# First v products early, DMA transposes in place of matmuls, and weights loaded once, in a one-core attention and gated-MLP kernel

## The chip, the cores and the metric

The kernel runs on one core of a Trainium2 chip. The metric is the device time of one execution in microseconds (us). The profile names the engines: PE (matrix products), PEld (its weight loads, beside PE), DVE (vector), ACT (scalar), POOL, and SP, which here only issues transfers. A "span" in a profile is some 1.7 to 2 us shorter than the timed execution.

## The reference, cut to what matters

```python
x = A_x                                    # 2048 tokens x 1024
xn = _layernorm(x, axis=-1)
s = _A_ref(xn, A_wqkv, A_wo)               # 32 heads, 8 keys per query at distances 0, 2, .. 14
g = _silu(_B_ref(xn, B_w1, B_w3, B_w2))    # silu(xn@w1) * (xn@w3) @ w2, inner size 3584
return x + s * g
```

## The kernel before

All large products are done by a Winograd form of Strassen's scheme: seven products of half size in place of eight, from sums of operands that DVE makes. PE is nearly always busy; everything else is arranged around it. Tokens come in four blocks of 512. Two blocks are the two halves of a Strassen product, so the sums of tokens (`xs`) need the second block normalized and transposed as well. Two of a product's seven parts need the first block alone. They are done first, for q and k, and their results parked (`snap`):

```python
for t, (w0, w1_, ws) in enumerate(((wq0, wq1, sq), (wk0, wk1, sk))):
    first_two(f"f{t}", [qkv_A(w0, w1_, ws, g) for g in range(2)], B0[0], B0[1],
              snap[2 * t:2 * t + 2], [qkv_copy(t, 0, 2 * g) for g in range(2)],
              *((lambda: None, 4) if t == 0 else (lambda: tp1(2, 3), 0)))   # tp1: transposes by matmuls
    if t == 0:
        tp1(0, 1)
```

Then follow the other five parts of q and k, all seven of v, the same for the second two blocks, and the MLP. One group of seven goes like this (cut):

```python
def seven(key, A, B, e11, e12, e22, e21, snap=None):
    ...                              # pa: a11*b11, pe: s1*t1; pb starts as a copy of pa
    e11(pa)                          # in the MLP: ACT writes silu(pa) into h_sb
    flush()
    for i in I:
        mm(pb[:, i], s2[i], t2, False)
    su2 = k4(f"u{key}")
    act_copy(su2[:], pb[:])          # ACT, in its order behind e11's activation
    for i in I:
        mm(pe[:, i], s4[i], b22, False)
    e12(pe, su2)
    run_hooks()
    for i in I:
        mm(pb[:, i], s3[i], t3, False)   # adds to pb: must wait for the copy above
    e22(pb, sp5)
```

The outputs of q, k and v for later blocks go through small buffers (`k4`, four of them) to HBM.

## Time and profile before

| | before |
|---|---|
| time, median of 6 runs | 732.54 us (732.24 to 732.9) |
| span of the profiled run | 730.3 us |
| PE busy | 714.2 us, 98% |
| DVE busy | 624.2 us, 85% |

Lines of this profile stand in the prediction below. The columns are start and end, length, busy time of PE, PEld, DVE, ACT and POOL (with the number of instructions), granted clock of PE, DMA share and GB/s:

```profile
600.00:700.00 100.00, 99.74 (x460) 45.38 (x464) 92.46 (x79) 25.27 (x25) 12.12 (x20) 1.00 0.51 160
```

PE is busy for all but 0.26 us there, and DVE for 92 of 100. It is the attention of the last block that DVE does beside PE.

### The profile page before, as it was taken

The page shows a single profiled execution, that of the slowest core. Times are in us where ns is not written, and L with a number is a line of the kernel's source. Part 1 is how long each engine was busy: PE and PEld are TensorE (multiplying, and loading weights), DVE is VectorE, ACT ScalarE, POOL GpSimd, SP SyncE. Part 2 cuts the span into 40 slices and gives each one's busy share as a digit, 9 for nine tenths or more (in the row PEclk, how much of TensorE's full clock was granted, in tenths as well). Part 3 has the DMA queues.
Part 4 walks back from the last instruction along what each step waited for, and adds up shares of the span by engine and source line. Part 5 has one row for each costly group of instructions (what it writes and reads, how often), then busy time and mean ns, then how long its engine had stood idle before and what let it go on. Part 6 is the DMA issues. An engine that isn't in the chain of part 4 may idle for free.

```text
span 730.3 us, 8739 instructions
## 1 busy us (share of the span) xinstructions
PE 714.2 (98%) x3312; PEld 345.8 (47%) x3367; DVE 624.2 (85%) x677; ACT 314.5 (43%) x328; POOL 99.3 (14%) x159
## 2 busy tenths in 40 slices
PE   7999999999999999999999999999999999999996
PEld 4655665654444444444444444444444444444442
DVE  7994688878798879878989899969859999979984
ACT  5744343437554546654545411123454555120233
POOL 0000000010400110142202010010345000510011
PEclk9999999999999999999999999999999999999999
DMA  9379148877756452467755745549799453666505
GB/s 321 140 177 286 57 147 281 254 210 262 200 204 231 143 175 87 141 194 242 231 174 191 240 156 186 178 162 375 188 283 326 136 159 102 192 190 203 179 5 111
DMA packets 117610, 140.82 MB, mean 193 GB/s; under 512 B 14273, under 2 KB 91073, under 8 KB 116929
## 3 DMA queue, kind: packets, MB, share of 16 engines
q1 hardware_dynamic: 103984, 101.47, 44.9%
q0 software_dynamic: 13584, 38.81, 17.2%
q8 instruction: 26, 0.43, 0.3%
q14 instruction: 16, 0.12, 0.1%
HBM read 98.30 MB, written 38.80 MB: 188 GB/s over the span
## 4 chain that ended last, share of the span: by engine, by line
PE 71%; DVE 18%; DMA 4%; issue 3%; ACT 3%; SPq 1%; POOL 0%; DVEq 0%; ACTq 0%; POOLq 0%
PE bm L149 17%; PE am L149 11%; PE em L149 11%; PE db L149 7%; PE bq L149 5%; PE de L149 4%; DVE pt L410 4%; PE eq L149 4%; PE da L149 3%; PE aq L149 3%; PE wb L149 2%; DVE pt L412 2%; PE we L149 2%; PE wa L149 2%; DMA q_dram<-pk 1%
## 5 line engine op out<-in xcount | busy, mean ns | idle before, releaser
L149 PEld LDWEIGHTS <-wring 128*128 128x128 f16 (+1 forms) x1920 | 201.7, 105 | 216.4 <-issue 5.2
L149 PEld LDWEIGHTS <-h_sb 128*128 128x128 f16 (+1 forms) x1088 | 114.0, 105 | 121.7 <-issue 1.0
L149 PE MATMUL bm<-xs,wring 128*128 128x512 f16 x504 | 117.3, 379 | 0.5 <-DVE h_sb L661 0.3
L149 PE MATMUL am<-xT,wring 128*128 128x512 bf16 x322 | 78.8, 379 | 0.9
L410 DVE TENSOR_TENSOR pt<-qt,kT 128x4096 bf16<-128x4096 bf16 x32 | 73.2, 2288 | 0.7
L149 PE MATMUL db<-wring,h_sb 128*128 128x512 f16 x336 | 73.2, 379 | 0.0
L465 DVE TENSOR_TENSOR BC<-Ep,vT 128x2048 bf16<-128x2048 bf16 x56 | 67.0, 1218 | 0.2
L646 DVE TENSOR_TENSOR um<-em,um 128x1024 f32<-128x1024 f32 x28 | 34.2, 1222 | 19.9 <-PE em L149 12.9
L648 ACT ACTIVATE g<-um 128x1024 bf16<-128x1024 f32 x28 | 29.6, 1057 | 49.7 <-DVE um L646 49.7
L149 PE MATMUL da<-wring,h_sb 128*128 128x512 bf16 x219 | 48.9, 379 | 0.3
L451 POOL DMA_DIRECT2D Ep<-pb x64 | 37.9, 600 | 25.5 <-DVE pb L447 18.5
L149 PE MATMUL bm<-h_sb,wring 128*128 128x512 f16 x168 | 39.7, 379 | 0.0
L149 PE MATMUL em<-xs,wring 128*128 128x512 f16 x168 | 39.7, 379 | 0.0
L412 DVE TENSOR_TENSOR pt<-pt 128x2048 bf16<-128x2048 bf16 x32 | 39.1, 1221 | 0.5
L475 DVE TENSOR_TENSOR oT<-oT,BC 128x2048 bf16<-128x2048 bf16 x32 | 39.1, 1220 | 0.5
L149 PE MATMUL em<-xT,wring 128*128 128x512 bf16 x161 | 39.2, 379 | 0.3
L159 ACT COPY bm<-am 128x1024 f32<-128x1024 f32 x28 | 28.0, 999 | 26.1 <-PE am L149 26.1
L159 ACT COPY pm<-em 128x1024 f32<-128x1024 f32 x28 | 28.4, 1013 | 19.3 <-PE em L149 19.2
L159 ACT COPY um<-bm 128x1024 f32<-128x1024 f32 x28 | 28.4, 1013 | 18.6 <-PE bm L149 18.2
L667 ACT CAST g<-bm 128x1024 bf16<-128x1024 f32 x28 | 28.3, 1010 | 17.6 <-PE bm L149 17.6
L351 DVE TENSOR_TENSOR pk<-eq,uq 128x1024 bf16<-128x1024 f32 x12 | 14.7, 1222 | 23.7 <-PE eq L149 13.2
L661 DVE TENSOR_TENSOR h_sb<-bm,pm 128x1024 bf16<-128x1024 f32 x21 | 25.6, 1218 | 5.3 <-PE bm L149 5.3
(176 smaller groups left out, 965.3 us busy)
## 6 DMA issues: line engine op xcount, KB each, us to landing
wring<-in_B_w_dram SPq DMA_DIRECT2D x61, 512.0 KB, 4.4
wring<-t_dram SPq DMA_DIRECT2D x16, 512.0 KB, 5.1
t_dram<-wring POOLq DMA_DIRECT2D x14, 512.0 KB, 4.5
wring<-in_A_wqkv_dram SPq DMA_DIRECT2D x6, 1024.0 KB, 8.0
wring<-t_dram SPq DMA_DIRECT2D x16, 384.0 KB, 5.5
wring<-in_B_w_dram SPq DMA_DIRECT2D x12, 384.0 KB, 4.7
wring<-in_A_x_dram SPq DMA_DIRECT2D x16, 256.0 KB, 6.1
Ep<-pb POOLq DMA_DIRECT2D x64, 64.0 KB, 4.9
```

The costliest lines, as they stand in the source:

```text
L149: anchor["pe"] = nc.tensor.matmul(ps, lhsT=lhs[k], rhs=rhs[k], start=(first and k == 0), stop=(k == n - 1), skip_group_check=not first,)
L159: nc.scalar.copy(out=out_, in_=in_)
L351: anchor["v"] = nc.vector.tensor_add(d, ps[:], a[0][:])
L410: nc.vector.tensor_mul(p_t[:], q[:], kT[:, :, o:o + CH])
L412: nc.vector.tensor_add(p_t[:, 0:4, :], p_t[:, 0:4, :], p_t[:, 4:8, :])
L451: nc.gpsimd.dma_start(out=pr[c][r:P:NR, :, sq * P:(sq + 1) * P], in_=pb[sq * 32:(sq + 1) * 32, :, :])
L465: nc.vector.tensor_mul(dst, E[:, w, :].unsqueeze(1).to_broadcast([P, n, CH]), vT[:, js, o:o + CH])
L475: nc.vector.tensor_add(A, A, B if w0 else C)
L646: v = nc.vector.tensor_add(su2[:], pe[:], su2[:])
L648: nc.scalar.activation(out=hl["g"][:, :, CH:], in_=su2[:], func=ACTF.Silu)
L661: anchor["v"] = nc.vector.tensor_add(h[:, :, CH:], pb[:], sp5[:])
L667: nc.scalar.copy(out=hl["g"][:, :, 0:CH], in_=pb[:])
```

## The change

The intent is to fill PE while the second block is prepared, and to take work from PE and DMA.

1. v's first two products come early as well, with their own result buffer `vsn` and weights in two attention buffers `wve`.
2. Three of the second block's four tiles are transposed by DMA, one by matmuls.
3. The v and q weights are loaded once. The second q sums are made from the first ones.
4. q's outputs for the last two blocks go to free rows of `h_sb` in place of small buffers. Outputs for block 1 are stored from POOL's queue.

The core of the diff (cut):

```diff
+    spare = [0, 1, 2, 3, 10, 11, 0, 1]
     def park(t, c, j0, name):
-        tl = k4(name, (2, CH), BF16)
+        tl = k4(name, (2, CH), BF16)[:] if t or c < 2 else rows(spare.pop(0), 1).rearrange(...)
...
-            nc.sync.dma_start(out=dst, in_=tl[:])
+            (nc.gpsimd if c == 1 else nc.sync).dma_start(out=dst, in_=tl)
...
+    TPE = (3,)
+    qkv_load(2, 0, wve[0][:])
+    for st in range(NST):
+        ln_dve(1, [st])
+        if st not in TPE:
+            for a, d in ((0, b12), (1, xT[:, 2])):
+                nc.sync.dma_start(out=d[:, :, st * P:(st + 1) * P], in_=xt[1][:, st, a * CH:(a + 1) * CH], transpose=True)
+        if st == 1:
+            qkv_load(2, 1, wve[1][:])
...
-    for t, (w0, w1_, ws) in enumerate(((wq0, wq1, sq), (wk0, wk1, sk))):
+    for t, (w0, w1_, ws) in enumerate(((wq0, wq1, sq), (wk0, wk1, sk), (wve[0][:], wve[1][:], sk))):
...
-    wq0 = qkv_load(0, 0, slot(8, (4, D)))
-    wq1 = qkv_load(0, 1, rows(0, 4).rearrange("p (k n) -> p k n", k=4))
-    qkv_sums(wq0, wq1, sk)
+    qkv_sums(wq0, wq1, sk, True)
```

More of the change, by code (lines that the diff above doesn't have):

```diff
@@ L305, with qkv_sums @@
     B0 = B_of(xT[:, 0], xT[:, 1], xT[:, 2], xs)
-    def qkv_sums(w0, w1_, st):
+    def qkv_sums(w0, w1_, st, again=False):
         lo = lambda w: w.rearrange("p k (c two j) -> p k c two j", two=2, j=4)[:, :, :, 0]
@@ L315, in qkv_sums @@
         s3 = hi(w0.bitcast(FP16))
+        if again:
+            nc.vector.tensor_sub(s2, a22, s3)
+            nc.vector.tensor_add(s1, s2, a11)
+            nc.vector.tensor_sub(s4, a12, s2)
+            pace["owed"] += 3.4
+            return
         nc.vector.tensor_add(s1, a21, a22)
@@ L329, in qkv_A @@
         return pick(v0, 0), pick(v1, 0), pick(v1, 1), sp(0), sp(1), pick(v3, 1), sp(2)
+    spare = [0, 1, 2, 3, 10, 11, 0, 1]
     def park(t, c, j0, name):
-        tl = k4(name, (2, CH), BF16)
+        tl = k4(name, (2, CH), BF16)[:] if t or c < 2 else rows(spare.pop(0), 1).rearrange("p (j n) -> p j n", j=2)
         dst = (q_dram, k_dram, v_dram)[t][c, :, j0:j0 + 2, :]
         def fin():
-            nc.sync.dma_start(out=dst, in_=tl[:])
-        return tl[:], fin
+            (nc.gpsimd if c == 1 else nc.sync).dma_start(out=dst, in_=tl)
+        return tl, fin
     def qkv_dst(t, c, j0):
@@ L405, in scores @@
         if c not in sc:
-            sc[c] = att_tile((W, CH), BF16, f"Es{c}"), att_tile((NJ, CH), BF16, f"pt{c}")
+            sc[c] = att_tile((W, CH), BF16, f"Es{c}"), oT[:, 0] if c == 0 else att_tile((NJ, CH), BF16, f"pt{c}")
         E, p_t = sc[c]
@@ L558 @@
     tiles = {}
-    free = [0, 1, 2, 3, 4, 6, 7, 8, 9]
+    free = [8, 9, 0, 1, 4, 2, 3, 6, 7]
     half = [0, 1]
@@ L971 @@
         (ln_act if st == 2 else ln_dve)(0, [st])
+    wve = [att_tile((4, D), BF16, f"wve{h}") for h in I]
+    vsn = att_tile((2, 2, CH), FP32, "vsn")
     qt[0] = att_tile((NJ, CH), BF16, "qt0")
@@ L982 @@
     sk = [sk[:, q] for q in range(3)]
-    b12 = k4("b12", (KH, CH), BF16)
+    b12 = rows(12, 2).rearrange("p (k n) -> p k n", k=KH)
+    TPE = (3,)
[4 more added lines that the diff above has]
+            for a, d in ((0, b12), (1, xT[:, 2])):
+                nc.sync.dma_start(
+                    out=d[:, :, st * P:(st + 1) * P], in_=xt[1][:, st, a * CH:(a + 1) * CH], transpose=True,
+                )
+        if st == 1:
+            qkv_load(2, 1, wve[1][:])
     x_load(2)
-    ln_dve(1, [0, 1])
-    ln_dve(1, [2, 3])
     sq = rows(20, 6, FP16).rearrange("p (q k n) -> p q k n", q=3, k=4)
@@ L993, in tp1 @@
         for st in sts:
-            ln_tp(1, st, [(b12[:].unsqueeze(1), slice(0, 1)), (xT[:, 2:3], slice(1, 2))])
-    for t, (w0, w1_, ws) in enumerate(((wq0, wq1, sq), (wk0, wk1, sk))):
+            ln_tp(1, st, [(b12.unsqueeze(1), slice(0, 1)), (xT[:, 2:3], slice(1, 2))])
+    snap += [vsn[:, 0], vsn[:, 1]]
+    for t, (w0, w1_, ws) in enumerate(((wq0, wq1, sq), (wk0, wk1, sk), (wve[0][:], wve[1][:], sk))):
         first_two(f"f{t}", [qkv_A(w0, w1_, ws, g) for g in range(2)], B0[0], B0[1],
                   snap[2 * t:2 * t + 2], [qkv_copy(t, 0, 2 * g) for g in range(2)],
-                  *((lambda: None, 4) if t == 0 else (lambda: tp1(2, 3), 0)))
-        if t == 0:
-            tp1(0, 1)
+                  *((lambda: None, 4), (lambda: None, 0), (lambda: tp1(*TPE), 0))[t])
     qkv_sums(wq0, wq1, sq)
-    xn_sums(xT[:, 0], xT[:, 1], b12[:], xT[:, 2], xs)
+    xn_sums(xT[:, 0], xT[:, 1], b12, xT[:, 2], xs)
     qkv_sums(wk0, wk1, sk)
@@ L1012 @@
     tr(2)
-    wv = [slot(2 + 4 * h, (4, D)) for h in I]
+    wv = [wve[h][:] for h in I]
     sva = slot(0, (2, 4, CH), FP16)
@@ L1019, in before_v @@
         if g == 0:
-            for h in I:
-                qkv_load(2, h, wv[h])
             tr(3)
-        else:
             with behind("v"):
@@ L1034 @@
     pace["n"] = PACE[0]
-    qkv_seven(2, 0, *wv, sv, step0)
+    qkv_seven(2, 0, *wv, sv, step0, snap[4:6])
     pace["n"] = PACE[1]
```

## The prediction

> **What bounds the kernel now.** I read the page's busy shares first, then the tensor engine's (PE's) waits, then the windows by stage, then the timeline of the first 90 us, where the change is.
>
> ```profile
> PE 714.2 (98%) x3312; PEld 345.8 (47%) x3367; DVE 624.2 (85%) x677; ACT 314.5 (43%) x328; POOL 99.3 (14%) x159
> ...
> PE tp L280 <- DVE wring L254: 2.3, 1, 2.3
> PE warm L141 <- DVE warm L138: 1.3, 1, 1.3
> PE am L149 <- ACT bm L159: 0.7, 1, 0.7
> PE eq L149 <- DVE xs L294: 0.5, 1, 0.5
> PE zp L425 <- DVE dsu L823: 0.5, 1, 0.5
> PE bq L149 <- DVE pk L351: 0.3, 1, 0.3
> ```
> The first line is the page's: PE works in 714.2 of 730.3 us. Below are the first rows of its waits (total, times, longest): after the start nothing lasts a microsecond. So 16.1 us are idle, and the windows tell where:
> ```profile
> 0.00:13.25 13.25, 9.04 (x55) 4.30 (x57) 9.21 (x25) 7.47 (x15) 1.81 (x13) 1.00 0.86 295
> 13.25:20.20 6.95, 6.95 (x33) 4.59 (x33) 6.94 (x17) 3.85 (x6) 0.00 (x0) 1.00 1.05 388
> 20.20:29.57 9.37, 8.78 (x65) 6.16 (x64) 9.37 (x12) 8.88 (x15) 0.00 (x0) 1.00 0.56 192
> 63.50:87.90 24.40, 23.90 (x109) 14.19 (x110) 14.16 (x12) 10.01 (x10) 0.00 (x0) 1.00 0.43 111
> 140.00:200.00 60.00, 58.67 (x272) 29.76 (x276) 46.85 (x61) 32.78 (x32) 12.83 (x21) 1.00 0.75 234
> ```
> Columns: length, then busy time of PE, PEld, DVE, ACT and POOL, clock, DMA share, GB/s. PE is idle for 4.2 us before its first product (13.25 us), 0.6 in the stage that prepares the second block, 0.5 in the k/v stage, 1.3 at the step to the MLP, and (a window not shown) 5.9 after 700 us. The change touches neither the first nor the last. Between 13 and 700 us it can win only PE work taken away, and some 6 us of small gaps.
>
> The timeline of PE, the first pieces of that stage (start, length, engine, line, operation):
> ```profile
> 13.25 7.07 PE L149 MATMUL af<-xT,wring 128*128 128x512 bf16 x32
> 20.15 1.06 PE L280 MATMUL tp<-ident,wring 128*128 128x128 bf16 x16
> 24.50 1.06 PE L280 MATMUL tp<-ident,wring 128*128 128x128 bf16 x16
> 25.40 3.62 PE L149 MATMUL af<-xT,h_sb 128*128 128x512 bf16 x16
> 29.57 2.35 PE L149 MATMUL eq<-xs,h_sb 128*128 128x512 f16 x10 [0.54 <-DVE xs L294]
> ```
> Two rates come from here. The 32 products of q run from 13.25 to 20.15: 6.90/32 = 0.2157 us each. Two tiles of transposes (16 matmuls) hold the queue from 24.50 to 25.40: 0.90/16 = 0.056 us each, 0.45 us a tile. The last row is the wait that the change aims at: k's first products end at 25.40 + 3.62 = 29.02, and the next product waits until 29.57 for xs, the differences of the first two token blocks, which need the second block normalized and transposed.
>
> **What the Trainium skill says.** "Perfetto Trace Analysis", Identifying the Most-Contended Engine: matmul busy time is a poor measure of distance to the peak, as matmuls are pipelined; the weight loads' share is better. The trace agrees in part: a matmul's mean duration is 379 ns where starts are 216 ns apart, and PEld is 47%. But with no gaps in the starts, the number of matmuls sets the time here. "VectorE: DVE Perf Modes", The three transpose paths: a 128x128 transpose takes 390 ns on TensorE and 1309 ns by DMA. The trace differs for a stream: 56 ns from one to the next on PE. A DMA transpose of a whole 128x1024 tile occupies the issuing queue for 1.32 us (median of 8) and lands 3.5 us after issue (3.0 to 8.2). "DMA: Bandwidth & Descriptors", Issuing engines are not separate DMA queues: moving an issue to another engine saves only sequencer time. That matters here, as the sync queue is blocked behind transposes (below).
>
> **The change, part by part.**
>
> *Removed from PE.* Three tiles x 8 transposing matmuls: 24 x 0.056 = **1.35 us**, wholly on the path, since PE has no gap around them. With them go six ACT evacuations of 0.61 us (3.7 us; ACT is 8.9 of 9.4 us busy in 20.2 to 29.57, but doesn't set the end).
>
> *Moved on PE.* The first two v products (32 matmuls, 6.9 us) leave the later v stage and come before q's remaining ones. PE's sum doesn't change. The gain is time for the second block: q's first products 13.25 to 20.15, k's to 27.05, v's, with one tile's 0.45 us in the middle, to 34.4. xs must then be ready at 34.4 instead of 29.0. DVE before it needs four normalizations (some 8 to 9 us), q's four sums (4 x 1.22 = 4.9) and the first xs (1.2): 15 us of the 22 after 12.6 us. So xs waits on data, not on DVE.
>
> *Added to DMA.* Before, DMA is at its limit until about 22 us (share 1.04 to 1.06, 381 to 406 GB/s in each microsecond from 9 to 21); wk1, the last weight, is issued by 9.3 us and lands about 21 to 22.5. Behind it now come v's first half (1 MB, 2.8 us at 385 GB/s), two transposed tiles, v's second half (2.8), the third tile. In 46 to 49 us the share is 0.61 + 0.99 + 0.91 = 2.5 for two tiles and a store, so I take 1.2 us a tile. Estimates: v's first half 25 (needed 27.05), second half 30 (needed 30.95), third tile 31.5 (needed for xs by 33.2). The margins are 1 to 2 us: everything fits, barely. Then the 0.54 us wait goes, and 0.1 around the second xs: **0.6 us**.
>
> *The k/v stage.* DVE waits 6.35 us at 55.8 for a k store to free its buffer; the store stood in the sync queue behind transposes of the last block, of which one held the queue 3.32 us. PE then loses 0.34 us to "pk" and 0.2 beside it. Stores of token block 1 now go out on POOL's queue, and b12 no longer takes one of the four small buffers: **0.45 us**. The v weights' load at 49.4 us is only moved.
>
> *Reloads and sums.* Two reloads of 1 MB at 112 and 115.6 us go; PE never waited for them. The second q sums cost 3 DVE operations instead of 4: 1.2 us of DVE, off the path. Rows instead of small buffers for q's last outputs remove DVE's wait of 4.10 us at 144.9. DVE so comes 5 us earlier to the step to the MLP, where PE stands about 1.5 us between 166 and 180, behind ACT (a table load and an exponential that waited 2.53 us for DVE). I credit a third: **0.5 us**.
>
> *New cost.* The last two q outputs lie in rows 0 and 1, and the first MLP activation writes just these rows. It ran at 169.2; the last q store was issued at 165.97, and the q stores' median landing in that stretch is 5.1 us, so 171. ACT then stands about 2 us, its next copy ends about 173.4, and PE needs it at 172.1. I expect **0.6 us** (1.3 in full, about half as likely). v's snapshots add two ACT copies of 1.0 us, hidden.
>
> Sum: -1.35 - 0.6 - 0.45 - 0.5 + 0.6 = -2.3 us. 732.37 - 2.3 = 730.1; I say **730.0**.
>
> **The rivals.**
> 1. *DMA becomes the bound of the early stage.* v's halves and transposes arrive later than estimated, and PE stands in v's first products or still at xs. For it: rings full to 22 us, transposes of up to 3.3 us on the queue, margins of 1 to 2 us. Against it: x2's load, formerly here, gives way, and DMA was idle from 28 to 37 us. It would cost 1 to 3 us and eat the gain: 731 to 733.
> 2. *The attention work starts late.* The v weights and snapshot take three of the four large attention buffers, so scores need the snapshot's, and the next q fetch the weights'. Against it: scores began only at 89.6 us, paced by credits, and v's snapshot is read at about 80. DVE is 92% busy from 540 to 700 us, so lasting delay would show there: 731 to 735. I give it one in ten.
> 3. *All small gaps close and rows 0 and 1 are free in time.* 1.35 + 0.6 + 0.5 + 1.5 = 4 us: 728.4.
>
> **Range and chances.** A small gain is surest: 1.35 us of PE work is gone in any case. Rival 3 sets the lower end with a little for reordering (727.8), rival 1 or the new ACT wait the upper (732.5). The 2% mark is 14.6 us; all idle time between 13 and 700 us is 6, so faster by 2% is all but excluded; slower by 2% would take an attention backlog over many stages. Chances: faster 0.01, same 0.97, slower 0.02.
>
> **What would show it.** Right: 24 fewer matmuls; 8 transposing ones from the second block; v's first products at about 27 us without a gap; no PE wait for xs at about 34 us; no wait of DVE for k stores; PE's work in all shorter by 1.3 us. Wrong: a PE wait for v's weights or b12 between 27 and 36 us (rival 1); scores after 90 us, and new PE waits on DVE after 400 us (rival 2); the first MLP activation waiting for a q store (my new cost; if it doesn't, that term falls). If the time moves by over 3 us though the first 90 us are as said, the cause is in the step to the MLP or later, which I have only guessed.

## More of the kernel before

Attention on DVE runs in the background. At the end of a half block of v it copies the last 16 columns (the "halo") on POOL and lets POOL fetch the next half block:

```python
def halo(t, js):
    nc.gpsimd.tensor_copy(out=t[:, js, 0:HALO], in_=t[:, js, CH:CH + HALO])
...
def fetch_v(c, js):
    ...
    halo(vT, js)
    anchor["pool"] = nc.gpsimd.dma_start(out=vT[:, js, HALO:], in_=v_dram[c, :, js])
```

## The result, and the profile after

The changed kernel takes 736.37 us (median of 6 runs, 734.37 to 738.91), the kernel before 732.54. A ratio is the mean time of one kernel's fast runs over that of the other's in the same rounds, so it isn't quite the ratio of the medians. Here it is 1.0053, with a 95% interval of 1.0034 to 1.0073. The change made the kernel slower by half a per cent (the same, by the 2% mark), where I had predicted 730.0. The run with the kept profile is one of the slower of the six (737.33).

The page's first line, and the first PE waits of the changed kernel (total, times, longest):

```profile
PE 716.7 (97%) x3288; PEld 345.6 (47%) x3343; DVE 623.1 (85%) x678; ACT 314.7 (43%) x326; POOL 112.0 (15%) x171
...
PE de L149 <- ACT dsp L159: 2.7, 1, 2.7
PE bm L149 <- ACT um L159: 2.4, 1, 2.4
...
PE bq L149 <- DVE pk L359: 1.0, 2, 0.6
PE af L149 <- DMA wve<-in_A_wqkv_dram: 0.4, 1, 0.4
PE bq L149 <- DVE xs L295: 0.4, 1, 0.4
```

PE has 24 matmuls fewer and is nevertheless busy for 2.5 us more. Two waits stand out, each of more than 2 us, where the kernel before had none over 0.7 after its start. Busier with less work means slower matmuls, and the windows show the clock:

```profile
20.20:29.57 9.37, 9.32 (x44) 6.22 (x44) 8.51 (x9) 6.63 (x8) 0.00 (x0) 1.00 1.27 226
63.50:87.90 24.40, 24.30 (x112) 14.27 (x113) 15.14 (x15) 9.96 (x10) 2.71 (x5) 1.00 0.27 102
140.00:200.00 60.00, 57.25 (x259) 28.58 (x263) 47.58 (x60) 31.72 (x31) 10.03 (x18) 0.97 0.66 217
600.00:700.00 100.00, 97.03 (x439) 43.68 (x442) 90.42 (x75) 22.85 (x23) 16.54 (x20) 0.98 0.52 163
```

In the first two stages PE now is busy all the time, as hoped. In the last two it is idle for 2.8 and 3.0 us (1.3 and 0.3 before), and the mean granted clock falls to 0.97 and 0.98, from 1.00. Asked for the 3.41 us from 173.75 and from 685.75, the profile gives a granted clock of 0.50. So time was lost twice, once at the step to the MLP and once at the far end, where nothing was changed.

**The early stage** went as intended, with small flaws (PE's timeline: start, length, engine, line):

```profile
12.99 10.30 PE L149 MATMUL af<-xT,wring 128*128 128x512 bf16 x47
23.35 3.62 PE L149 MATMUL af<-xT,h_sb 128*128 128x512 bf16 x16
26.80 3.62 PE L149 MATMUL af<-xT,wve 128*128 128x512 bf16 x16
30.25 0.61 PE L280 MATMUL tp<-ident,wring 128*128 128x128 bf16 x8
31.31 3.67 PE L149 MATMUL af<-xT,wve 128*128 128x512 bf16 x15 [0.45 <-DMA wve<-in_A_wqkv_dram]
34.86 1.92 PE L149 MATMUL eq<-xs,h_sb 128*128 128x512 f16 x8
```

The products run through to 30.25 without a gap. Then PE waits 0.45 us for v's second half of weights, which stood behind four DMA transposes. At 34.86 there is no wait for `xs`.

**The stall at 171 us** (lines of several engines from one timeline):

```profile
164.69 0.32 SPq L344 DMA_DIRECT2D q_dram<-h_sb  x1
...
170.11 1.28 ACT L650 ACT_TABLE_LOAD   x1 [3.50 <-DMA q_dram<-h_sb]
...
171.40 1.02 ACT L650 ACTIVATE h_sb<-am 128x1024 bf16<-128x1024 f32 x1
172.32 1.01 ACT L159 COPY um<-bm 128x1024 f32<-128x1024 f32 x1
...
173.38 3.24 PE L149 MATMUL bm<-xs,wring 128*128 128x512 f16 x8 [2.41 <-ACT um L159]
```

The last two q outputs lie in rows 0 and 1 of `h_sb`; the last of their stores is issued at 164.69. The first MLP activation writes into both rows, so ACT waits for that store, 3.5 us. The wait stands before a table load of 1.28 us that precedes the activation, and the copy that PE needs is behind both on ACT. PE starts again at 173.38 instead of 170.81, and its next eight matmuls take 3.0 us, where eight take 1.73 elsewhere.

**The stall at 683 us**, first in the kernel before, then in the changed one (POOL and DVE timelines):

```profile
649.13 1.17 POOL L387 COPY vT<-vT 128x64 bf16<-128x64 bf16 x1 [16.27 <-DVE BC L465]
...
658.30 1.23 DVE L465 TENSOR_TENSOR oT<-Ep,vT 128x2048 bf16<-128x2048 bf16 x1 [4.65 <-DMA vT<-v_dram]
```

```profile
650.99 4.58 POOL L395 COPY vT<-vT 128x64 bf16<-128x64 bf16 x1 [30.34 <-DVE BC L473]
...
655.86 0.77 POOL L409 DMA_DIRECT2D vT<-v_dram  x1 [0.30 <-POOL vT L395]
...
663.12 1.23 DVE L473 TENSOR_TENSOR oT<-Ep,vT 128x2048 bf16<-128x2048 bf16 x1 [7.65 <-DMA vT<-v_dram]
...
682.17 1.22 DVE L822 TENSOR_TENSOR dsp<-db,dsp 128x1024 f32<-128x1024 f32 x1
...
685.43 4.87 PE L149 MATMUL de<-wring,h_sb 128*128 128x512 bf16 x14 [2.71 <-ACT dsp L159]
```

The tiny halo copy takes 4.58 us in place of 1.17. The load behind it lands later, and DVE gets to work at 663.1 instead of 658.3. With no slack, its addition `dsp` starts at 682.2 instead of 678.35. ACT waits for it, and PE for ACT. The Trainium skill's page "SBUF — State Buffer", Who interferes with whom, has a mechanism: a DVE instruction with two SBUF inputs contends with a GpSimd instruction that reads SBUF, and the port pair that they share is an exclusive lock. The trace agrees in so far as the copy starts 0.14 us after one of DVE's two-input operations and ends at 655.57, 0.1 us after the last of four such operations run back to back. The five other traces with the copy on POOL and this wait have it at 4.57 to 4.58 us too. Why it got in after one operation in the kernel before isn't shown by any run.

### The profile page after: what moved, and what is told of

Read it like the earlier page. It is cut to its first block, busy times and chain, and to the rows that moved or that the text cites. A ratio compares the mean times of both kernels' runs of the same rounds, so it can differ in the third digit from the quotient of the medians.

```text
span 735.6 us, 8693 instructions
## 1 busy us (share of the span) xinstructions
PE 716.7 (97%) x3288; PEld 345.6 (47%) x3343; DVE 623.1 (85%) x678; ACT 314.7 (43%) x326; POOL 112.0 (15%) x171
## 4 chain that ended last, share of the span: by engine, by line
PE 79%; DVE 7%; issue 5%; DMA 3%; ACT 3%; POOL 2%; SPq 0%; DVEq 0%; ACTq 0%; POOLq 0%
PE bm L149 18%; PE am L149 12%; PE em L149 12%; PE bq L149 8%; PE db L149 7%; PE eq L149 5%; PE de L149 4%; PE da L149 3%; PE aq L149 3%; PE wb L149 2%; PE af L149 2%; PE we L149 2%; DVE BC L473 2%; PE wa L149 1%; DMA wring<-in_A_x_dram 1%
## 5 line engine op out<-in xcount | busy, mean ns | idle before, releaser
L149 PEld LDWEIGHTS <-wring 128*128 128x128 f16 (+1 forms) x1824 | 188.4, 103 | 211.4 <-issue 7.7
L149 PEld LDWEIGHTS <-h_sb 128*128 128x128 f16 (+1 forms) x1056 | 109.9, 104 | 123.9 <-issue 6.8
L149 PE MATMUL bm<-xs,wring 128*128 128x512 f16 x504 | 118.8, 382 | 2.6 <-ACT um L159 2.4
L418 DVE TENSOR_TENSOR pt<-qt,kT 128x4096 bf16<-128x4096 bf16 x24 | 55.0, 2290 | 0.7
L958 POOL DMA_DIRECT2D out_dram<-h_sb x12 | 15.1, 1511 | 98.2 <-DVE h_sb L957 98.1
L420 DVE TENSOR_TENSOR pt<-pt 128x2048 bf16<-128x2048 bf16 x24 | 29.3, 1221 | 0.4
```

The lines of the kernel that those rows point to most:

```text
L149: anchor["pe"] = nc.tensor.matmul(ps, lhsT=lhs[k], rhs=rhs[k], start=(first and k == 0), stop=(k == n - 1), skip_group_check=not first,)
L418: nc.vector.tensor_mul(p_t[:], q[:], kT[:, :, o:o + CH])
L420: nc.vector.tensor_add(p_t[:, 0:4, :], p_t[:, 0:4, :], p_t[:, 4:8, :])
L958: nc.gpsimd.dma_start(out=rows_, in_=g, accum_op=ALU.add)
```

## The ledger

To compare kernels whose starts differ by up to a microsecond, I cut PE's timeline at four points: the first product of q, the first of the MLP (`am`), the product `db` in the last down projection (at 639.44 us in the kernel before), and the first product of the last output projection (`wa`). Each entry is the start of a group minus the one before:

| us | before | changed | rows 2, 3 | rows 2, 3 and halo | halo only |
|---|---|---|---|---|---|
| first product at | 13.25 | 12.99 | 12.30 | 12.55 | 13.19 |
| to `am` (q, k, v) | 148.21 | 147.22 | 145.68 | 146.05 | 146.42 |
| to `db` | 477.98 | 480.04 | 475.83 | 475.83 | 479.83 |
| to `wa` | 60.44 | 64.99 | 62.89 | 60.44 | 60.44 |
| to the end | 30.42 | 30.36 | 30.40 | 30.43 | 30.42 |
| span | 730.3 | 735.6 | 727.1 | 725.3 | 730.3 |

The last three columns are experiments below. The changed kernel's loss of 5.3 us is -0.26 - 0.99 + 2.06 + 4.55 - 0.06.

## The experiments

Theory A: q's outputs in rows 0 and 1 cause the stall at 171 us. Theory B: the halo copy on POOL causes the one at 683. Theory C: a part of each stall's cost is PE's slow clock after it. The rival to all: the loss comes from the early stage's DMA traffic or from the moved attention work.

### Other rows (e1_rows23)

```diff
-    spare = [0, 1, 2, 3, 10, 11, 0, 1]
+    spare = [0, 1, 2, 3, 10, 11, 2, 3]
```

> The last two q outputs go to rows 2 and 3 in place of 0 and 1; the order of instructions on every engine is that of the changed kernel. Theory A (the first MLP activation waits 3.5 us on ACT for a q store that still reads rows 0 and 1, the tensor engine stands 2.4 us for it and then runs its next 9 products at half speed): both waits go, the clock of 140 to 200 us is 1.00 again, and the time falls by 3 to 4.5 us, to about 732 to 733. If the wait at 683 us goes as well by the shift in time, 728. Rival (the loss is from the early stage or the moved attention work): no change, 736.

Measured: 730.39 us (728.79 to 731.43, 4 runs), ratio to before 0.9962 (0.9944 to 0.998). The order of instructions is the same on all engines, so only the rows differ. The activation no longer waits for a store (ACT's timeline):

```profile
164.39 1.28 ACT L650 ACT_TABLE_LOAD   x1
165.69 1.02 ACT L650 ACTIVATE h_sb<-am 128x1024 bf16<-128x1024 f32 x1
167.15 1.02 ACT L159 COPY um<-bm 128x1024 f32<-128x1024 f32 x1 [0.44 <-PE bm L149]
```

The copy now waits for PE, not PE for it. The stage to `db` falls from 480.04 to 475.83: the stall cost **4.21 us**. Theory A holds, and the rival falls for this part. The halo copy still took 4.57 us here and PE's wait at 677 us stayed. The time is 1.6 to 2.6 us below what I expected of the rows alone: in this one trace the early stage was better (145.68), and the second stall was not followed by slow matmuls.

### Other rows, and the halo copy on DVE (e2_rows23_halo)

```diff
-        nc.gpsimd.tensor_copy(out=t[:, js, 0:HALO], in_=t[:, js, CH:CH + HALO])
+        nc.vector.tensor_copy(out=t[:, js, 0:HALO], in_=t[:, js, CH:CH + HALO])
```

together with the edit above.

> As the run before, and the nine small halo copies of k and v go from the Pool engine to the vector engine. Theories A and B together (B: the Pool copy of the v halo at 651 us took 4.58 us in place of 1.2, so v's next half landed 5 us later, the vector engine waited 7.65 us and the tensor engine 2.7 us with a slow clock after it): no tensor engine wait over 1 us after 13 us, time 727 to 729, below the kernel before. If only A holds: 732.

Measured: 726.97 us (726.59 to 727.41), ratio to before 0.9917 (0.9901 to 0.9934). It beats both kernels: the change is worth 0.8% once its two stalls are gone. PE's waits, complete:

```profile
PE tp L280 <- DVE wring L254: 1.4, 1, 1.4
PE warm L141 <- DVE warm L138: 1.3, 1, 1.3
PE bq L149 <- DVE pk L359: 0.9, 2, 0.6
PE tp L280 <- ACT wring L274: 0.3, 1, 0.3
```

Three of them are before the first product. Only 0.9 us of listed waits remain after it.

### The halo copy on DVE alone (e4_halo)

The second edit only, on the changed kernel.

> The changed kernel, with only the nine halo copies moved to the vector engine; the rows stay. Theory B: the wait of the tensor engine at 683 us goes, the one at 171 us stays; time 731 to 732.5. If the wait at 683 comes from anything else (the order of the vector engine's work, later attention), it stays: 736.

Measured: 731.98 us (728.71 to 732.05), ratio 0.9974 (0.9951 to 0.9998). The stage to `wa` falls from 64.99 to 60.44, exactly that of the kernel before: the second stall cost **4.55 us**, and moving the copies removes it. The wait at 171 us stayed (2.2 us). That it does so by sparing POOL's long copy is not shown, for the edit has a second effect. With it the scheduler put the DVE operation that waits for the load two operations later in DVE's queue (POOL and DVE):

```profile
652.86 0.77 POOL L409 DMA_DIRECT2D vT<-v_dram  x1 [30.28 <-DVE vT L395]
...
661.63 1.23 DVE L473 TENSOR_TENSOR oT<-Ep,vT 128x2048 bf16<-128x2048 bf16 x1 [4.41 <-DMA vT<-v_dram]
...
678.16 1.22 DVE L822 TENSOR_TENSOR dsp<-db,dsp 128x1024 f32<-128x1024 f32 x1
```

Counted from `db`, the wait for the load ends after 18.86 us in the kernel before (658.30 - 639.44), 22.87 in the changed one and 22.19 here. So the load came only 0.7 us earlier than in the changed kernel: it was issued sooner, but took 8.8 us to land in place of 7.3. But the addition `dsp` came 3.2 us earlier (38.72 after `db`, against 41.92): the other 2.5 us are the two operations that went ahead of the wait. As the origin of the stall the copy is read from the two traces alone: between the kernel before and the changed one the load came 4.0 us later, of which the longer copy makes 3.4. A run with a short copy and DVE's order as it was would decide, and there is none.

The two edits work separately: 4.21 + 4.55 = 8.76 of the 10.3 us between the spans of the changed and the mended kernel. The other 1.5 us are in the first product's time (0.44) and the early stage (1.17), which vary from run to run.

### Dummy products in the gap (e3_fill)

```diff
-        run_hooks()
+        run_hooks(); key == "m0_0" and spin(bank2("fill"), 8)
```

> The changed kernel with eight dummy products of 512 columns put into the tensor engine's gap at 171 us, ahead of the product that waits. The ACT wait stays. Theory C (half of what the gap costs is the tensor engine's slow clock after it): the product after the gap still starts at about 173.4, but its eight matmuls take 1.7 us in place of 3.0, and the time falls by about 2 us although there is 1.7 us more work: 734. Rival (only the gap itself costs, the slow matmuls are a part of the wait): same or longer, 736 to 738.

Measured: 739.9 us (738.3 to 740.63), ratio 1.009. As a whole this missed, but in place the products run as theory C said:

```profile
175.81 1.89 PE L141 MATMUL fill<-warm 128*128 128x512 bf16 x8
177.82 1.89 PE L149 MATMUL bm<-xs,wring 128*128 128x512 f16 x8
179.54 1.89 PE L149 MATMUL am<-h_sb,wring 128*128 128x512 bf16 x8
```

The product after the gap starts at 177.82 and the next one 1.72 us later: full speed. As a test this is weak, though. In this run PE was free for the waiting product at 175.81 and the copy `um` ended at 177.77, so without the dummies the gap would have been about 2.0 us, and gaps of 1.9 and 2.15 us elsewhere in the same trace had no slow matmuls after them. What shows the slow clock is the changed kernel's own trace (0.50 for 3.41 us after each stall). There PE needed 5.14 us from the start of `bm` at 173.38 to `em` at 178.52, where two products take 3.45. So **1.7 us** of that stall was the slow clock, and the gap itself 173.38 - 170.81 = 2.57. Together that is 4.26, against the 4.21 of the ledger. The total got worse for another reason: with the extra buffer the scheduler exchanged two pairs of entries in the sync queue. At 110 us a k store now stands behind a weight load, and PE's wait for `pk` at 113 us grew from 0.6 to 1.6. Two new PE waits of 2.0 and 1.7 us appeared at 135 and 142 us, behind ACT and DVE operations that wait for v stores; how the new order leads to these I didn't trace. A total alone would have refuted a theory that the changed kernel's trace supports.

### The changed kernel again (r1_again, r2_again, r3_again)

> The changed kernel once more, for its trace alone. Its six timed runs lay between 734.4 and 738.9, the mended kernel's four within 0.8 us. Theory C (a gap of over 2 us can drop the tensor engine's clock for about 3 us, depending on when it falls): both waits (171 and 683 us) are there again with nearly the same length, and the times of the looks differ by the count of slow matmuls after them, 0 to 4 us. Rival (the waits themselves differ from run to run): the lengths of the two waits follow the time.

> As the look before: the same two waits, a time between 733 and 739 that follows the slow matmuls after them.

> As the two looks before: the same two waits, a time between 733 and 739 that follows the slow matmuls after them.

Measured: 735.82, 737.72 and 736.35 us, one look each (single runs on another chip, so their state is unknown). The waits at 171 us were 2.7, 2.4 and 2.9 us, those at 683 us 2.5, 2.7 and 3.2, and all were followed by slow matmuls. The stage to `db` was 480.19, 479.99 and 480.24, and to `wa` 64.78, 65.02 and 65.07. So both stalls are a fixed property of the program, and the slow matmuls don't explain the spread of these runs. That part of the expectation was wrong. What varied was the early stage (145.98, 147.61, 146.47): in the second PE waited 0.7 us for v's weights, in the first and third there was no such wait in the list.

### The halo copy in the kernel before (e5_before_halo)

The same halo edit on the kernel before.

> The kernel before, with only the nine halo copies on the vector engine. There the Pool copies took 0.2 to 1.3 us and the tensor engine had no wait from them, so theory B expects no change: within 0.5 us of before. If the vector engine's copies are worth something by themselves (a part of the 6 us that the mended change gains), up to 2 us faster.

Measured: 732.76 us, ratio 1.0004 (0.9986 to 1.0022). The halo edit was worth nothing in the kernel before, where POOL's copy happens to get in, so the mended kernel's gain belongs to the change. Its profiled run was the slowest of four (735.41), with a 2.0 us wait at 149 us that the profile of before hasn't; I didn't follow it.

### All four tiles by matmuls (e6_pe_tp)

```diff
-    TPE = (3,)
+    TPE = (0, 1, 2, 3)
```

on the mended kernel.

> The mended change (rows 2 and 3, halo on the vector engine, 727.0) with all four tiles of the second block transposed by matmuls again. My estimate for the part: 24 matmuls of 0.056 us are back, so plus 1.35 us if DMA was not in the way; less, if the six DMA transposes delay the v weights (0.45 us wait in the changed kernel's trace): plus 0.5 to 1. So 727.5 to 728.4. The three tiles' own ACT copies may delay xs: another 0.3.

Measured: 728.81 us (728.73 to 729.68, 5 runs), ratio 0.9945 (0.9932 to 0.9957). Against the mended kernel's 726.97 the three tiles by DMA are worth 1.8 us, a little above my range. The two came from different rounds; the intervals of their ratios to before, 0.9932 to 0.9957 and 0.9901 to 0.9934, just meet. In the traces the stage to `am` is 147.77 and 146.05: 1.72 us, of which 1.35 are the matmuls; the list has 0.2 us of wait for `xs`, too.

### q's outputs in small buffers again (e7_no_rows)

```diff
-        tl = k4(name, (2, CH), BF16)[:] if t or c < 2 else rows(spare.pop(0), 1).rearrange(...)
+        tl = k4(name, (2, CH), BF16)[:]
```

on the mended kernel (the rows edit drops out).

> The mended change with q's last outputs back in the small buffers. The wait of the first MLP activation must stay away (theory A: it is the rows that tie it to a store). The vector engine's wait of 4 us for q stores near 143 us comes back. My estimate of that part was 0.5 us on the path: 727.5; if it delays the step to the MLP as before, plus 1.5: 728.5.

Measured: 727.63 us (727.03 to 727.91), ratio 0.9925 (0.9911 to 0.9938). The interval overlaps that of the mended kernel, and the stages are alike (145.89, 475.82, 60.44). DVE waits for q stores 1.4 us in all, not 4. So the free rows gain nothing that I can measure, while in the form of the change they cost 4.2 us.

### All k and v stores from POOL (e8_allpool)

```diff
-            (nc.gpsimd if c == 1 else nc.sync).dma_start(out=dst, in_=tl)
+            (nc.gpsimd if c == 1 or t else nc.sync).dma_start(out=dst, in_=tl)
```

on the mended kernel.

> The mended change with the k and v stores of the second block on Pool's queue too. The tensor engine's wait of 0.63 us for pk at 112 us comes from a k store that stands behind a weight load on the sync queue; it should go: 726.3. Rival: Pool's queue is in order as well, and its t and Ep transfers come later for it: same or slower.

Measured: 727.35 us (726.64 to 728.25, 5 runs), ratio 0.9924 (0.991 to 0.9937): no difference. PE's wait for `pk` at 112 us is still 0.52 us, so a k store in the sync queue wasn't its cause. It stays unexplained.

## Why the prediction was wrong

**The gains were right, or too small.** Removed matmuls, the wait for `xs` and the k/v stage summed to 2.4 us. The stage to `am` gained 2.16 us in the mended kernel. In the changed kernel's own trace it gained 0.99, as rival 1 took a part: the four transposes before v's second half held the sync queue for 9.0 us, where I had read 1.32 each from the kernel before, and PE waits for that half (0.45) and for the second `xs` (0.44). For the step to the MLP and later I credited a third of 1.5 us; the stage to `db` shows 477.98 - 475.83 = 2.15 in the mended kernel. So all those gaps closed, as in rival 3. With both stalls away, rival 3's 728.4 was nearest. That the time with rows 2 and 3 alone, 730.39, is so near my 730.0 is luck: there the gains that I had put too low are offset by the second stall, which I had not foreseen.

**The new cost was the right mechanism and the wrong size.** The term "I expect 0.6 us (1.3 in full, about half as likely)" measured 4.21. Its parts are a gap of 2.57 us, where I had 1.3 in full, and 1.7 us of slow clock after it, for which I had no term. In the gap the step that failed is what stands behind the wait on ACT. I let the activation wait, and took its table load as done before (it ran at 167.87 there). In the changed kernel the table load waits too, and its 1.28 us come after the store has landed. The store took 5.4 us to land, against my 5.1. That the copy's end, 173.33, agrees with my 173.4 is luck: my figure was on the clock of the kernel before, and in the changed one both the store's issue (164.69 against 165.97) and PE's need (170.81 against 172.1) came 1.3 us earlier. And halving it for doubt had no ground: the same rows and the same order make it happen every time.

**The second stall had no term at all.** 4.55 us came from a stage some 510 us after the step to the MLP (171 to 683), where the source was not changed. I had named DVE's 92% load from 540 to 700 us under rival 2, but as lasting delay of the attention work. The delay was not inherited: the stage to `db` of the "rows 2, 3" kernel is already 2 us shorter than before, and the stall is still there. By the traces it is a short POOL copy that has to find a place between DVE operations, with a load and a DVE without slack behind it; the experiment removes the stall, but doesn't separate the copy from DVE's order. No number in the profile of before would have given its cost, but the chain was visible there: DVE waited 4.65 us for just this load.

**Rival 2** is not seen: at `db` the changed kernel's DVE work is no later than PE's own loss.

## What to carry to other kernels

When a buffer is reused, ask who writes it next and what sits behind that wait in the engine's queue: here a table load, the activation and the copy that PE needed. Take both arrival times from the *changed* schedule. Price a gap in PE of over 2 us with the slow matmuls after it, here 1.7 us more in most cases. When an edit removes a stall, compare the order of instructions too: it may have changed more than you meant. If a near-full kernel moves the wrong way, cut the timeline into stages and compare these: two stalls of 4 us in different places had hidden a gain of nearly 6.

## What the Trainium skill lacked or had wrong

- "TensorE: Matmul & The Clock Gate", Part 1, What's actually happening, says that the clock falls back after an idle window of about 3.4 us, and that the window is free-running. Here gaps of 2.37 (halo only), 2.57 and 2.88 us (changed kernel) were enough for 3.41 us at half the clock, some eight matmuls at 0.43 us in place of 0.216, while one of 2.46 us (rows 2, 3; from 676.11 to 678.57) had no slow matmul after it. Of all 13 gaps of over 2 us after the start in the traces here, 11 were followed by the slow clock, the shortest of 2.19 us (halo edit in the kernel before, at 147 us). That fits a window that runs freely, but not a length of 3.4 us of full idleness.
- "SBUF — State Buffer", Who interferes with whom: that the shared port is an exclusive lock is there, not that one engine may lose it through several operations in a row, as it looks here. A copy of 128 x 64 elements took 4.57 to 4.58 us beside four of DVE's back-to-back operations, and 1.17 beside one.
- "VectorE: DVE Perf Modes", The three transpose paths, has the time of one transpose by each path, not what moving it is worth in a busy kernel: three 128x1024 tiles moved from PE to DMA gained 1.8 us, of which 1.35 are 24 matmuls at 0.056 us.
